# Layer 1's second product: earlier weight conversions, a third float64 tile, g loaded four steps ahead

## The chip, the core and the metric

The kernel runs on one core of a Trainium2 chip. The metric is the device time of one execution in microseconds (us). Five engines have a queue each and work through it in order: PE (TensorE, the matmuls; PEld is its weight load), DVE (VectorE), ACT (ScalarE), POOL (GpSimd) and SP (SyncE, here an issuer of DMAs). ACT issues DMAs too. An instruction that waits holds up all that is queued behind it on its engine.

## The reference

Attention with a sigmoid in place of the softmax, then two feed-forward layers over 1,792 tokens of 768 features, with 2,048 hidden features each:

```python
def _attn_ref(q, k, v):
    scores = scale * np.matmul(q, k.transpose(0, 1, 3, 2)) - np.log(S)
    attn = 1.0 / (1.0 + np.exp(-scores))
    return np.matmul(attn, v)

def _moe_ref(x, w_in, w_out):
    h = x @ w_in
    g = h * (1.0 / (1.0 + np.exp(-h)))
    return g @ w_out

def _moe2_ref(x, w_in, w_out, a, b):
    h = x @ w_in
    P = a[0] + a[1] * h + a[2] * h * h + a[3] * h ** 3
    Q = 1.0 + np.abs(b[0]) * np.abs(h) + np.abs(b[1]) * h * h
    return (P / (Q + 1e-06)) @ w_out
```

q, k and v are (4, 12, 448, 64): B = 4 batches of S = 448 tokens. The four weight matrices arrive as float64 numbers, and the kernel handles them as pairs of 32-bit words.

## The kernel before

**Precision.** A float32 operand is split into a high part (a cast to fp32r) and the low rest, and each product is three matmuls: high by high, high by low, low by high. `split` (L286) and `split2` (L290) make the high part on ACT (L287, L291) and the low part on DVE (L288, L292); `split_later` and `flush` (L296, L300) put the low parts behind other DVE work (L302).

**Conversions.** The weights come as 64 tiles of float64, 32 for each layer, each 768 KB. `conv` (L141) takes the oldest staged tile, makes float32 of it with one ACT instruction (L150) and four DVE instructions (L151, L152, L153, L156), stores the result of 384 KB to DRAM (L159, on SP) and issues the load of the next float64 tile (`conv_load`, L126, also on SP) into the staging tile it has freed. There are two staging tiles (`NST`). The order of the tiles is fixed: 16 of w_in1, 16 of w_out1, then layer 2's 32. Later the float32 tiles are loaded again: w_in1 into `wf` by `load_w1` (SP), w_out1 into `wos` by `load_wo1` (ACT's queue), layer 2's by `load_w2`.

**Stages.** First comes attention, 24 steps i. Then layer 1's first product by Strassen's scheme in 16 steps g of seven products each (`p1` to `p7`, L423 for the matmuls); step g sums and splits the weights for the next one (`sums_12`, `prep_...`) and loads those of g + 2. The silu of a result goes to DRAM as `gd`. Then layer 1's second product, which is where most of the change lies: 64 steps n, batch b = n // 16 by slice c = n % 16 of the hidden features. `second(n)` is 18 matmuls of 128x448 (L559 to L561), six groups that each add to one PSUM bank. In the first batch (the first block, n = 0 to 15) each step also needs its weights split (`split_wo1`), which stay in SBUF from then on. At the end of a block (n = 15, 31, 47, 63) `results1` copies six results from PSUM to SBUF and stores them as `xs`. Layer 2 follows, in which no weight is converted.

**Order of a step of the second product.** The code issues `load_g(n + 2)` (224 KB of `gd` into one of the nine `f448` slots, DMA on ACT's queue, L525), then `second(n)`, then `split_gd(n + 1)` (ACT L287, DVE L288), in the first block also `split_wo1(n + 1)` and `load_wo1(n + 5)`, then `results1` if a block ends, then `conv_to`, which converts as many tiles as an even pace asks for. At n = 2 `both`, `c21` and `c12` finish the first product's last results. At n = 49 the first loads for layer 2 are issued (four `load_w2`, three `load_x`); from n = 52 on each step holds a `split_x`, and two steps a `split_w` on POOL.

**How many conversions where.** 18 in attention, 10 in the Strassen steps (g = 0, 2, 4, 6 and 10 to 15), and 36 in the second product, n = 3 to 58 at an even pace, 9 of them in the first block: the last four of w_out1 and all of layer 2's.

The nine f448 slots and the staging tiles are rings: the slot that was put back first is taken first, whatever still reads it; the new user then waits.

Of the kernel before, what the change touches and what calls it, by code (L numbers as in the profile page):

```python
# [41 lines left out]
def attention_moe_moe(ctx: ExitStack, tc: tile.TileContext, q, k, v, w_in1, w_out1, w_in2, w_out2, a, b2, out):  # L42
# [23 lines left out]
    def fixed(nm, n, shape, dt, pool=cpool):  # L66
        return [pool.tile(shape, dt, tag=f"{nm}{i}", name=f"{nm}{i}") for i in range(n)]
# [10 lines left out]
    f_all = cpool.tile([P, 9 * S], F32, tag="f", name="f")  # L78
    f448 = Ring([f_all[:, i * S : (i + 1) * S] for i in range(9)])
    f2 = Ring([f_all[:, i * 2 * S : (i + 1) * 2 * S].rearrange("p (j s) -> p j s", j=2) for i in range(4)])  # L80
    xio = Ring(fixed("xio", 3, [P, BK], F32))
    stage = Ring(fixed("stg", NST, [P, DM, 2], I32))
    bits = Ring(fixed("bits", 3, [P, DM], F32))
    xs = [[dr_p.tile([P, NT], F32, tag=f"xs{m}_{d}", name=f"xs{m}_{d}") for d in range(KD)] for m in range(2)]
# [80 lines left out]
    def conv_to(count):  # L165
        while done["conv"] < min(count, len(order)):
            conv()
# [353 lines left out]
    def load_g(n):  # L521
        if n < B * KF:
            b, c = divmod(n, KF)
            gq[n] = f448.get()
            nc.scalar.dma_start(out=gq[n], in_=gd[c][b])  # L525

    def split_gd(n):
        if n < B * KF:
            t = gq.pop(n)
            gx[n] = hl.get()  # L530
            split(t, gx[n])
            f448.put(t)
# [4 lines left out]
    def load_wo1(c):  # L537
        if c < KF:
            wo_in[c] = wos.get()
            nc.scalar.dma_start(out=wo_in[c], in_=wd[0][c]["o"])  # L540

    def split_wo1(c):
        if c < KF:
            t = wo_in.pop(c)
            split2(t, woH[c], woL[c])
            wos.put(t)
# [6 lines left out]
    def second(n):  # L553
        b, c = divmod(n, KF)
        x = gx.pop(n)
        for d in range(KD):
            o = ybank(b, d)
            w = slice(d * P, (d + 1) * P)
            nc.tensor.matmul(o, woH[c][:, w], x[:, 0, :], start=(c == 0), stop=False)  # L559
            nc.tensor.matmul(o, woH[c][:, w], x[:, 1, :], start=False, stop=False)  # L560
            nc.tensor.matmul(o, woL[c][:, w], x[:, 0, :], start=False, stop=(c == KF - 1))  # L561
        hl.put(x)
# [15 lines left out]
    def load_w2(kind, c):  # L578
        nc.sync.dma_start(out=slot(kind, c), in_=wd[1][c][kind])
# [19 lines left out]
    def split_x(g, d):  # L599
        w = blocks[g][1]  # L600
        t = xf.pop((g, d))
        x = hx.get()
        nc.scalar.copy(x[:, 0, :w], t[:, :w])
        nc.vector.tensor_tensor(out=x[:, 1, :w], in0=t[:, :w], in1=x[:, 0, :w].bitcast(F32), op=ALU.subtract)
        xio.put(t)
        xs_hl[g, d] = x
# [136 lines left out]
    with tc.manual_schedule():  # L743
# [36 lines left out]
        for i in range(NPT):  # L780
            for h in range(2):
                if h == 0:
                    mix(i + 2)
                    load_v(i + 3)
                    load_qk(i + 4)
                attn_S(i, 2 * h, attn_QK(i, 2 * h))
                p = attn_QK(i, 2 * h + 1)
                if h == 0:
                    if i == 0:
                        attn_T(1, "k")  # L790
                    attn_T(i + 1, "q")
                else:
                    hl.put(st.pop(("k", i)), st.pop(("q", i)))
                    attn_T(i + 2, "k")
                attn_S(i, 2 * h + 1, p)
                behind(*((i, 0) if h else (i - 1, 1)))
                at_half = 2 * i + h - 2 * NPT
                if at_half >= -NOPS - 6:
                    next(first_ops, None)
                flush()  # L800
                if at_half == -8:
                    load_w1(0)
                    load_w1(1)
                if at_half == -5:
                    xk_s.close()
                    wr_p, wr_s = opened("wr")
                    wr.extend(fixed("wr", 4, [P, DM], F32R, wr_p))
                    wq.extend(fixed("wq", 6, [P, HM], F32R, wr_p))
                    prep_ij(0)
                    sums_12(0)  # L810
                if at_half == -3:
                    prep_s12(0)
                if at_half == -1:
                    prep_a22(0)
                if h == 0 and 0 < i < NPT - 5:
                    conv()
        for _ in first_ops:
            pass
# [25 lines left out]
        for g in range(NGR):  # L844
            was = g >= 1

            p1(g)
            flush()
            if was:
                keep(g - 1, "u3")  # L850
            if g >= 2:
                c12(g - 2)
            if g == HF:
                operands1_late("T3")
            if g == HF + 1:
                operands1_late("22")

            p2(g)
            flush()
            keep(g, "s1")  # L860
            if was:
                both(g - 1, "u3", "c")
            sums_34(g)
            if g == HF - 1:
                operands1_late("T2")

            if was:
                p4(g - 1)
                c22(g - 1)
            flush()  # L870
            both(g, "s1", "b")
            sums_12(g + 1)
            if was:
                fill(g)
            if g in (0, 2, 4, 6) or g > HF + 1:
                conv()

            p6(g)
            flush()
            c11(g)  # L880
            if was:
                c21(g - 1)
            prep_s3(g)
            if g == HF - 1:
                operands1_late("T1")
            if g == HF:
                operands1_late("T4 sums")
            if g == last:
                for n in range(4):
                    load_g(n)  # L890

            p5(g)
            flush()
            keep(g, "r")
            prep_ij(g + 1)
            if g:
                prep_a22(g)
            fill(g)
            if g == HF:
                operands1_late("T4")  # L900
            if g == last:
                split_wo1(0)
                load_wo1(4)
                split_gd(0)

            if was:
                p3(g - 1)
            flush()
            load_w1(g + 2)
            if g == HF - 1:  # L910
                operands1_late("T3 sums")
            if g == last - 1:
                kt_s.close()
                wos_p, wos_s = opened("wos", side="right")
                wos.put(*fixed("wos", 4, [P, DM], F32, wos_p))
                for c in range(4):
                    load_wo1(c)
            if g == last:
                split_wo1(1)
                load_wo1(5)  # L920
                split_gd(1)

            p7(g)
            flush()
            if was:
                both(g - 1, "r", "c")
            prep_s12(g + 1)
            prep_s4(g)
# [17 lines left out]
        split_wo1(2)  # L946
        load_wo1(6)
        split_gd(2)
        NL1 = B * KF
        todo = len(order) - done["conv"]  # L950
        for n in range(2, NL1):
            load_g(n + 2)
            second(n)
            if n == 2:
                c21(last)
                both(last, "r", "c")
                c12(last)
            split_gd(n + 1)
            if n + 1 < KF:
                split_wo1(n + 1)  # L960
                load_wo1(n + 5)
            if n == KF - 1:
                wos_s.close()
                l2_p = ctx.enter_context(tc.tile_pool(name="l2a", bufs=1, side="right", reuse_waits="tile"))
                hx.put(*fixed("hx", KD, [P, 2, BK], F32R, l2_p))
                wi_f.extend(fixed("wif", 4, [P, DM], F32, l2_p))
            if n % KF == KF - 1:
                results1(n // KF)
            conv_to(len(order) - todo + todo * (n - 1) // (NL1 - 7))
            m = n - (NL1 - KF)  # L970
            if m == 1:
                whr.put(w0[:2], w0[2:])
                for c in range(4):
                    load_w2("i", c)
                for d in range(HK):
                    load_x(0, d)
            if 4 <= m < 4 + KD:
                split_x(0, m - 4)
                if m - 4 < HK:
                    load_x(0, m - 4 + HK)  # L980
            if m in (KF - 6, KF - 4):
                split_w("i", (m - KF + 6) // 2)
        assert done["conv"] == len(order)
        wo_s.close()
        xa_s.close()
        l2_p = ctx.enter_context(tc.tile_pool(name="l2b", bufs=1, reuse_waits="tile"))
# [16 lines left out]
        wo_f.extend(slots["o", c] for c in range(KF))  # L1003
        whr.put(more_wh[:2], more_wh[2:])
        for t in list(stage.free):
            t = t.bitcast(F32).rearrange("p e t -> p (e t)")
            xio.put(*(t[:, i * BK : (i + 1) * BK] for i in range(2 * DM // BK)))
        for c in range(KF):
# [40 lines left out]
```

## Time and profile before

| | us |
|---|---|
| median of three runs | 1128.04 |
| lowest and highest of the runs | 1127.06, 1131.84 |
| the profiled execution | 1133.58 |
| its span in the trace | 1131.8 |
| attention until about | 182 |
| the Strassen product until | 387.13 |
| the second product, to the end of its last step | 658.62 |
| layer 2 until | 1131.8 |

The rows that are needed stand in a section of their own below. The page's busy times tell which engine has no time to spare over the span; the windows tell that for a stage; the waits tell what an engine stood still for; the timeline names single instructions, with the idle time before them and what ended it in brackets.

### The profile page before, as it was taken

What the parts mean: (1) busy time and instruction counts of PE and PEld (TensorE: products, weight loads), DVE (VectorE), ACT (ScalarE), POOL (GpSimd) and SP (SyncE); (2) the same over time, 40 slices, a digit from 0 to 9 for tenths busy, and PEclk for the clock granted to TensorE, in tenths of its full rate; (3) what the DMA queues carried; (4) which work ended last, traced back from release to release, by engine and by line L of the source; (5) the groups of instructions that cost most, each with busy time, mean ns of one, the idle gap of its engine ahead of it and who ended that gap; (6) DMA issues with size and microseconds to landing.
All of it is one profiled execution on the core that took longest, in us unless ns stands there. A gap on an engine that the chain in (4) does not pass through costs nothing.

```text
span 1131.8 us, 15809 instructions
## 1 busy us (share of the span) xinstructions
PE 1096.3 (97%) x5822; PEld 913.8 (81%) x5822; DVE 862.2 (76%) x1028; ACT 636.3 (56%) x1035; POOL 341.8 (30%) x246
## 2 busy tenths in 40 slices
PE   9999999999999898999998899999999999999997
PEld 5554456999998787889987788888999888889997
DVE  4668855778876747767675758888999988798996
ACT  6778885666655533323322345546666765566664
POOL 2111210000000000000000136656777666566774
PEclk9999999999999999999999999999999999999999
DMA  9999962766556848888889573010101010001001
GB/s 253 261 263 248 286 216 98 256 211 212 168 191 216 280 165 285 266 280 277 302 270 330 173 285 154 1 35 8 57 1 47 12 41 1 29 15 56 1 1 42
DMA packets 100349, 177.96 MB, mean 157 GB/s; under 512 B 8368, under 2 KB 74416, under 8 KB 100272
## 3 DMA queue, kind: packets, MB, share of 16 engines
q1 hardware_dynamic: 88048, 155.38, 42.7%
q10 hardware_dynamic: 12160, 21.57, 5.9%
q8 instruction: 46, 0.75, 0.3%
q14 instruction: 31, 0.25, 0.1%
q0 software_dynamic: 64, 0.00, 0.0%
HBM read 123.31 MB, written 53.61 MB: 156 GB/s over the span
## 4 chain that ended last, share of the span: by engine, by line
PE 80%; DVE 8%; DMA 7%; ACT 2%; issue 2%; ACTq 1%; SPq 0%; POOL 0%; DVEq 0%; POOLq 0%
PE acc L690 14%; PE acc L423 10%; PE acc L693 7%; PE hb L621 7%; PE hb L619 7%; PE hb L620 7%; PE hb L264 6%; PE pair L246 5%; PE hb L423 4%; PE acc L560 3%; PE acc L561 3%; PE acc L559 3%; DMA f<-gd 3%; PE hb L236 2%; DVE bits L153 1%
## 5 line engine op out<-in xcount | busy, mean ns | idle before, releaser
L292 POOL TENSOR_TENSOR w<-wif,w 128x768 fp32r<-128x768 f32 x33 | 62.0, 1879 | 486.5 <-ACT w L291 482.0
L257 ACT ACTIVATE f<-pair,nls 112x896 f32<-112x896 f32 x96 | 96.7, 1012 | 26.8 <-PE pair L246 26.8
L560 PE MATMUL acc<-xa,woH 128*128 128x448 f32 x252 | 94.3, 374 | 5.5 <-DVE xa L288 5.5
L559 PE MATMUL acc<-xa,woH 128*128 128x448 f32 x252 | 93.9, 372 | 3.6 <-ACT xa L287 3.5
L561 PE MATMUL acc<-xa,woL 128*128 128x448 f32 x252 | 93.4, 371 | 0.0
L150 ACT ACTIVATE bits<-stg 128x768 f32<-128x768 f32 x64 | 57.7, 902 | 63.3 <-DMA stg<-in_moe_w_in_dram 38.7
L647 DVE RECIPROCAL stg<-stg 128x512 f32<-128x512 f32 (+1 forms) x28 | 84.9, 3032 | 0.0
L634 ACT ACTIVATE stg<-hb,absb 128x512 f32<-128x512 f32 (+1 forms) x44 | 28.0, 637 | 98.2 <-PE hb L621 98.2
L264 PE MATMUL hb<-f,vs 112*64 112x448 f32 x384 | 82.5, 551 | 0.0
L287 ACT CAST xa<-f 128x448 fp32r<-128x448 f32 x64 | 36.0, 562 | 81.6 <-DMA f<-gd 65.9
L246 PEld LDWEIGHTS pair<-xa,xa 64*112 64x112 f32 x576 | 47.2, 173 | 38.5 <-issue 32.4
L246 PE MATMUL pair<-xa,xa 64*112 64x448 f32 x576 | 71.7, 381 | 0.0
L423 PE MATMUL acc<-xb,wr 128*128 128x448 f32 x315 | 67.8, 366 | 0.0
L292 POOL TENSOR_TENSOR wh<-wif,wh 128x768 fp32r<-128x768 f32 x31 | 57.4, 1851 | 26.4 <-DVE xio L639 23.6
L151 DVE TENSOR_SCALAR bits<-bits 128x768 f32<-128x768 f32 x64 | 35.7, 557 | 37.9 <-ACT bits L150 37.6
L156 DVE SCALAR_TENSOR_TENSOR bits<-stg,bits 128x768 int32<-128x768 int32 x64 | 62.8, 981 | 2.2
L423 PEld LDWEIGHTS acc<-xb,wr 128*128 128x128 f32 x315 | 59.0, 188 | 5.5 <-issue 0.7
L153 DVE SCALAR_TENSOR_TENSOR bits<-stg,bits 128x768 int32<-128x768 int32 x64 | 61.4, 959 | 2.2
L288 DVE TENSOR_TENSOR xa<-f,xa 128x448 fp32r<-128x448 f32 x64 | 39.0, 620 | 30.1 <-ACT xa L287 30.1
L690 PE MATMUL acc<-w,hx 128*128 128x512 f32 x174 | 61.4, 393 | 0.0
L690 PE MATMUL acc<-wh,hx 128*128 128x512 f32 x171 | 60.3, 393 | 0.0
L292 POOL TENSOR_TENSOR w<-wof,w 128x768 fp32r<-128x768 f32 x32 | 59.3, 1852 | 0.4 <-ACT w L291 0.2
(195 smaller groups left out, 3188.8 us busy)
## 6 DMA issues: line engine op xcount, KB each, us to landing
stg<-in_moe_w_in_dram SPq DMA_DIRECT2D x32, 768.0 KB, 6.4
stg<-in_moe_w_out_dram SPq DMA_DIRECT2D x32, 768.0 KB, 6.2
gd<-f SPq DMA_DIRECT2D x64, 224.0 KB, 4.9
f<-gd ACTq DMA_DIRECT2D x64, 224.0 KB, 4.5
wf<-w0i SPq DMA_DIRECT2D x32, 384.0 KB, 6.0
w0i<-bits SPq DMA_DIRECT2D x16, 384.0 KB, 2.9
w0o<-bits SPq DMA_DIRECT2D x16, 384.0 KB, 2.6
wos<-w0o ACTq DMA_DIRECT2D x16, 384.0 KB, 4.6
```

Of the source, the lines that this page charges most:

```text
L246: nc.tensor.matmul(p[:CP, j, :S], K[rows[j], a_, c * CP : (c + 1) * CP], Q[rows[j], b_, :], start=(n == 0), stop=(n == 2),)
L257: nc.scalar.activation(t[:CP], p[:CP, :, :S], AF.Sigmoid, bias=nls[:CP], scale=QKSCALE)
L264: nc.tensor.matmul(pav[0][j * D : (j + 1) * D, :S], vs[i][:, j, c * D : (c + 1) * D], t[:CP, j], start=(c == 0), stop=(c == NCH - 1),)
L292: (eng or nc.vector).tensor_tensor(out=lo, in0=src, in1=h.bitcast(F32), op=ALU.subtract)
L423: nc.tensor.matmul(o, w_[:, w], x[:, i_, :], start=first and kk == 0 and n_ == 0, stop=kk == HK - 1 and n_ == 2, skip_group_check=not first,)
L559: nc.tensor.matmul(o, woH[c][:, w], x[:, 0, :], start=(c == 0), stop=False)
L560: nc.tensor.matmul(o, woH[c][:, w], x[:, 1, :], start=False, stop=False)
L561: nc.tensor.matmul(o, woL[c][:, w], x[:, 0, :], start=False, stop=(c == KF - 1))
L619: nc.tensor.matmul(o, wh[:, w], x[:, 0, :wd_], start=first, stop=False)
L620: nc.tensor.matmul(o, wh[:, w], x[:, 1, :wd_], start=False, stop=False)
L647: nc.vector.reciprocal(t0, t1)
L690: nc.tensor.matmul(acc[t][:, :BK], a_, w_[:, :BK], start=first, stop=last)
```

## The change

**Conversions.** Attention holds two more (i = 19, 20), the Strassen steps two more (g = 1 and g = 9), so that 32 are done ahead of the second product: all of layer 1's. In the second product three stand in the first block (n = 5, 9, 13), and 29 in n = 17 to 51: every step but n = 22, 27, 32, 37, 42 and 47. Thus 32 instead of 36, and none behind n = 51.

**A third float64 tile.** The three `xio` tiles are allocated as one, and that stands in as a third staging tile (`more`) from n = 2 on, until layer 2's `load_x` takes the three tiles back.

**Loads of g.** `load_g(n + 4)` instead of `load_g(n + 2)`; two more are issued ahead of the loop.

**Order.** At n = 2 the splits for n = 3 stand ahead of `c21`, `both` and `c12`. `load_x` starts at n = 53 instead of 49, `split_x` at n = 55 instead of 52; `load_w2` stays.

```diff
-    xio = Ring(fixed("xio", 3, [P, BK], F32))
+    x_all = cpool.tile([P, 3, BK], F32, tag="xio", name="xio")
+    xio = Ring([x_all[:, i, :] for i in range(3)])
...
-                if h == 0 and 0 < i < NPT - 5:
+                if h == 0 and 0 < i < NPT - 3:
                     conv()
...
-            if g in (0, 2, 4, 6) or g > HF + 1:
+            if g in (0, 1, 2, 4, 6) or g > HF:
                 conv()
...
+        load_g(4)
+        load_g(5)
         NL1 = B * KF
-        todo = len(order) - done["conv"]
+        more = x_all.rearrange("p a b -> p (a b)").bitcast(I32).rearrange("p (e t) -> p e t", t=2)
+        stage.put(more)
+        conv_load()
+        first, slow, end = done["conv"], KF - 2, NL1 - 12
+
+        def conv_by(n):
+            if n <= KF:
+                return first + (n - 1) // 4
+            return first + slow // 4 + -(-(n - KF) * (len(order) - first - slow // 4) // (end - KF))
+
         for n in range(2, NL1):
-            load_g(n + 2)
+            load_g(n + 4)
             second(n)
+            split_gd(n + 1)
+            if n + 1 < KF:
+                split_wo1(n + 1)
+                load_wo1(n + 5)
             if n == 2:
                 c21(last)
                 both(last, "r", "c")
                 c12(last)
-            split_gd(n + 1)
-            if n + 1 < KF:
-                split_wo1(n + 1)
-                load_wo1(n + 5)
...
-            conv_to(len(order) - todo + todo * (n - 1) // (NL1 - 7))
+            conv_to(conv_by(n))
             m = n - (NL1 - KF)
...
             if m == 1:
                 whr.put(w0[:2], w0[2:])
                 for c in range(4):
                     load_w2("i", c)
+            if m == 5:
                 for d in range(HK):
                     load_x(0, d)
-            if 4 <= m < 4 + KD:
-                split_x(0, m - 4)
-                if m - 4 < HK:
-                    load_x(0, m - 4 + HK)
+            if 7 <= m < 7 + KD:
+                split_x(0, m - 7)
+                if m - 7 < HK:
+                    load_x(0, m - 7 + HK)
```

From L81 on the lines of the changed kernel are one higher, so L151 there is L150 here. PE's order is unchanged.

DVE in the Strassen step g = 1, before: the last two sums of the next weights (`sf`), the low part of an operand (`xa`), the low part of `wq`, which p7 of this step reads, and the next operand.

```order
L309 TENSOR_TENSOR sf_253<-wf_1_250 128x384
L306 TENSOR_TENSOR sf_253<-sf_253,wf_0_249 128x384
L288 TENSOR_TENSOR xa_216<-T_1957,xa_216 128x448
L302 TENSOR_TENSOR wq_1844<-sf_254,wq_1843 128x384
L288 TENSOR_TENSOR xa_219<-xio_63,xa_219 128x448
```

The same place now:

```order
L310 TENSOR_TENSOR sf_251<-wf_1_248 128x384
L307 TENSOR_TENSOR sf_251<-sf_251,wf_0_247 128x384
L289 TENSOR_TENSOR xa_214<-T_1969,xa_214 128x448
L152 TENSOR_SCALAR bits_64<-bits_64 128x768
L153 TENSOR_SCALAR bits_64<-bits_64 128x768
L154 SCALAR_TENSOR_TENSOR bits_64<-stg_63,bits_64 128x768
L157 SCALAR_TENSOR_TENSOR bits_64<-stg_63,bits_64 128x768
L303 TENSOR_TENSOR wq_1856<-sf_252,wq_1855 128x384
L289 TENSOR_TENSOR xa_217<-xio,xa_217 128x448
```

A whole conversion stands between `xa` and `wq`. Its store and the 768 KB load that follows it also come ahead of the next weights' loads (`wf`) in SP's queue.

ACT in the first block, before: three steps, each with the high part of g (`xa`), the high part of the weights (`woH`), the load of later weights (`wos`) and of a later g (`f<-gd`); the first of the three steps has a conversion (`bits`).

```order
L287 CAST xa_220<-f 128x448
L291 CAST woH_3660<-wos_3462 128x768
L540 DMA wos_3462<-w0o_162 128x768
L150 ACTIVATE bits_67<-stg_64 128x768
L525 DMA f<-gd_0_105 128x448
L287 CAST xa_221<-f 128x448
L291 CAST woH_3662<-wos_3463 128x768
L540 DMA wos_3463<-w0o_164 128x768
L525 DMA f<-gd_0_109 128x448
L287 CAST xa_222<-f 128x448
L291 CAST woH_3664<-wos_3464 128x768
L540 DMA wos_3464<-w0o_166 128x768
```

The same engine in the same block now:

```order
L288 CAST xa_218<-f 128x448
L292 CAST woH_3686<-wos_3488 128x768
L541 DMA wos_3488<-w0o_160 128x768
L526 DMA f<-gd_0_111 128x448
L288 CAST xa_219<-f 128x448
L292 CAST woH_3688<-wos_3489 128x768
L541 DMA wos_3489<-w0o_162 128x768
L526 DMA f<-gd_0_115 128x448
L288 CAST xa_220<-f 128x448
L292 CAST woH_3690<-wos_3490 128x768
L541 DMA wos_3490<-w0o_164 128x768
```

None of these three steps has a conversion now, and `f<-gd` is for two steps further on.

ACT at the end of the first block, before: three of the six copies of `results1` (to slots `f_60`), then the loads of g for n = 18, 19 and 20 with the high parts for n = 17 and 18.

```order
L567 COPY f_60<-hb0_281 128x448
L567 COPY f_60<-acc1_1967 128x448
L567 COPY f_60<-acc3_1969 128x448
L525 DMA f_60<-gd2_1_90 128x448
L287 CAST xa8_224<-f_60 128x448
L150 ACTIVATE bits0_66<-stg0_64 128x768
L525 DMA f_60<-gd3_1_94 128x448
L287 CAST xa0_216<-f_60 128x448
L150 ACTIVATE bits1_67<-stg1_65 128x768
L525 DMA f_60<-gd4_1_98 128x448
```

Now:

```order
L568 COPY f_60<-hb0_279 128x448
L568 COPY f_60<-acc1_1979 128x448
L568 COPY f_60<-acc3_1981 128x448
L526 DMA f_60<-gd4_1_96 128x448
L288 CAST xa8_222<-f_60 128x448
L526 DMA f_60<-gd5_1_100 128x448
L288 CAST xa0_214<-f_60 128x448
L151 ACTIVATE bits2_66<-stg0_62 128x768
L526 DMA f_60<-gd6_1_104 128x448
```

The first load behind the copies is that of n = 20 (`gd4_1`), and it takes the slot from which `results1` stores its first result; before, the load of n = 20 stood two steps later. The high part for n = 17 is queued behind it, and in the later blocks those for n = 33 and n = 49 likewise.

## Rows read from the trace of the kernel before

**Rows 1.** The page: busy time of each engine over the span.

```profile
PE 1096.3 (97%) x5822; PEld 913.8 (81%) x5822; DVE 862.2 (76%) x1028; ACT 636.3 (56%) x1035; POOL 341.8 (30%) x246
```

**Rows 2.** Windows: bounds, length; busy us (instructions) by engine; clock, DMA share, GB/s.

```profile
387.13:467.07 79.94, 68.86 (x307) 59.39 (x307) 51.25 (x71) 30.86 (x48) 0.00 (x0) 0.96 0.68 229
467.07:529.07 62.00, 60.17 (x289) 53.84 (x288) 41.09 (x59) 18.34 (x30) 0.00 (x0) 1.00 0.84 275
529.07:588.59 59.52, 59.52 (x289) 54.06 (x288) 40.90 (x59) 18.39 (x30) 0.00 (x0) 1.00 0.86 288
588.59:658.62 70.03, 62.20 (x290) 54.96 (x288) 40.95 (x56) 20.84 (x35) 4.61 (x2) 0.98 0.71 238
658.62:1131.80 473.18, 466.34 (x2497) 413.49 (x2495) 414.12 (x342) 284.82 (x490) 304.56 (x190) 1.00 0.14 46
```

**Rows 3.** Waits of PE, second product: line, releaser, total us, times, longest.

```profile
PE acc L560 <- DVE xa L288: 6.1, 8, 2.4
PE hb L560 <- DVE xa L288: 4.7, 5, 1.3
PE acc L559 <- ACT xa L287: 3.5, 1, 3.5
PE hb L559 <- DVE f L309: 2.8, 1, 2.8
```

**Rows 4.** Timeline, DVE and PE, first block: start, duration, instruction [idle before].

```profile
411.89 0.56 DVE L151 TENSOR_SCALAR bits<-bits 128x768 f32<-128x768 f32 x1 [1.32 <-ACT bits L150]
...
414.95 0.62 DVE L288 TENSOR_TENSOR xa<-f,xa 128x448 fp32r<-128x448 f32 x1
415.49 0.95 DVE L292 TENSOR_TENSOR woL<-wos,woH 128x768 fp32r<-128x768 f32 x1
...
410.41 0.36 PE L559 MATMUL hb<-xa,woH 128*128 128x448 f32 x1
...
414.06 0.36 PE L559 MATMUL hb<-xa,woH 128*128 128x448 f32 x1
415.62 0.47 PE L560 MATMUL hb<-xa,woH 128*128 128x448 f32 x1 [1.20 <-DVE xa L288]
```

**Rows 5.** Timeline of ACT, first block: conversions of two steps running.

```profile
420.08 0.89 ACT L150 ACTIVATE bits<-stg 128x768 f32<-128x768 f32 x1 [1.40 <-DVE woL L292]
...
425.95 0.91 ACT L150 ACTIVATE bits<-stg 128x768 f32<-128x768 f32 x1 [2.44 <-DVE woL L292]
```

**Rows 6.** Windows of 10 us, columns as in rows 2.

```profile
536.00:546.00 10.00, 10.00 (x50) 9.09 (x49) 6.59 (x11) 2.76 (x5) 0.00 (x0) 1.00 0.92 330
616.00:626.00 10.00, 9.54 (x36) 7.83 (x36) 4.96 (x8) 5.17 (x9) 0.00 (x0) 0.83 0.85 302
666.00:676.00 10.00, 9.18 (x46) 7.40 (x45) 9.89 (x8) 7.31 (x12) 8.27 (x5) 1.00 1.03 401
```

**Rows 7.** Timeline of ACT and PE: the longest wait of block four.

```profile
613.96 0.62 ACT L603 CAST hx<-xio 128x512 fp32r<-128x512 f32 x1 [5.58 <-DMA xio<-xs]
...
615.10 0.47 PE L559 MATMUL acc<-xa,woH 128*128 128x448 f32 x1 [3.53 <-ACT xa L287]
```

**Rows 8.** Waits of PE in attention, then in the Strassen product.

```profile
PE hb L236 <- DVE xa L239: 2.7, 5, 0.6
...
PE hb L423 <- DVE wq L302: 1.3, 1, 1.3
```

**Rows 9.** Timeline of DVE and PE at g = 1 of the Strassen product.

```profile
203.21 0.62 DVE L288 TENSOR_TENSOR xa<-T,xa 128x448 fp32r<-128x448 f32 x1
203.75 0.55 DVE L302 TENSOR_TENSOR wq<-sf,wq 128x384 fp32r<-128x384 f32 x1
...
204.07 0.98 PE L423 MATMUL hb<-xa,wq 128*128 128x448 f32 x4
```

**Rows 10.** results1's stores (L568): first ones of block two; all, issue to landing.

```profile
527.75 2.42 SPq L568 DMA_DIRECT2D xs<-f  x4
...
DMA to landing us min/median/max: 1.9/6.1/8.4
```

More of the change, by code (lines that the diff above doesn't have):

```diff
@@ L968, in attention_moe_moe @@
                 results1(n // KF)
-            conv_to(len(order) - todo + todo * (n - 1) // (NL1 - 7))
+            conv_to(conv_by(n))
             m = n - (NL1 - KF)
+            if m == 4:
+                assert done["conv"] == len(order)
             if m == 1:
@@ L974, in attention_moe_moe @@
                     load_w2("i", c)
+            if m == 5:
                 for d in range(HK):
                     load_x(0, d)
-            if 4 <= m < 4 + KD:
-                split_x(0, m - 4)
-                if m - 4 < HK:
-                    load_x(0, m - 4 + HK)
+            if 7 <= m < 7 + KD:
+                split_x(0, m - 7)
+                if m - 7 < HK:
+                    load_x(0, m - 7 + HK)
             if m in (KF - 6, KF - 4):
                 split_w("i", (m - KF + 6) // 2)
-        assert done["conv"] == len(order)
         wo_s.close()
@@ L1005, in attention_moe_moe @@
         for t in list(stage.free):
+            if t is more:
+                continue
             t = t.bitcast(F32).rearrange("p e t -> p (e t)")
```

## The prediction, made before the changed kernel was run

> **What bounds the kernel now.** I read the page's busy times first. PE is busy 97% of the span, and the next engine, DVE, 76% [rows 1]: time can be won only where PE waits, or where its matmuls run slowly. The windows by stage come next. After 658.62 PE is busy 466.34 of 473.18 us [rows 2], and the change leaves that stage alone. The stretch to look at is the second product, 387.13 to 658.62. There I need the price of a step with nothing late: steps 4 and 5 begin 3.65 us apart, at 410.41 and 414.06 [rows 4]. A block of 16 steps is then 58.4 us. The first block also holds two products of the stage before, which have the matmuls of one step: 62.05. Measured are 79.94, 62.00, 59.52 and 70.03 us [rows 2], so the blocks lose 17.9, 3.6, 1.1 and 11.6 us, **34.2 us in all**. That is the most that the second product can give.
>
> What is lost, and to whom, the waits of PE tell. Nearly all are for operands on their way through ACT and DVE: the low part of g (L288) 6.1 and 4.7 us, its high part (L287) once for 3.5, and 2.8 at the start for the sum `f` that frees a PSUM bank [rows 3]. The clock is the rest: the window that begins a microsecond after the wait of 3.5 us shows 0.83 of full speed over 10 us, so (1 - 0.83) x 10 = 1.7 us more [rows 6].
>
> **The first block.** The timeline shows what a conversion does. Its four DVE instructions run from 411.89 to the `xa` at 414.95, 3.06 us, and only then come the low parts that PE needs; PE stands for 1.20 us at 415.62 [rows 4]. On ACT the conversion's first instruction begins only once the low weights are done, at 420.08 and, a step later, at 425.95 [rows 5]: two steps with conversions running are 5.87 us apart. Less the 3.06 us, a step without one is about 2.8, under PE's 3.65. So each conversion in this block puts the chain 5.87 - 3.65 = 2.2 us behind, and each free step wins 0.85 back. Nine conversions in the 13 steps from n = 3 would cost 9 x 2.2 - 4 x 0.85 = 16.4, less the lead that g had. Of 17.9 us lost, 2.8 + 1.7 = 4.5 is the start (wait and clock), which the change doesn't touch, and 13.4 comes from this. Three conversions four steps apart fall behind by 2.2 and win 3 x 0.85 = 2.6 back; with g loaded two steps earlier PE should hardly stand. I leave 1.2 us (0 to 4).
>
> **The other blocks.** Block two loses 3.6 and block three 1.1; of that I leave 1.7, since the matmuls of block three run 3.72 us a step, without waits [rows 2], and that remains. In block four two things go: the high part of g for n = 54 is queued on ACT behind a `split_x` whose load is late by 5.58 us, and PE waits 3.53 [rows 7], with 1.7 of slow clock after it; and a conversion late in the block, beside the first splits on POOL, makes PE wait 2.4 [rows 3]. The changed kernel has no conversion after n = 51 and starts the `split_x` three steps later. I leave 0.3.
>
> **A new wait at the ends of blocks.** The order of ACT shows the load for n = 20, 36 and 52 right behind the copies of `results1`, into the slot whose store was just issued. ACT stands until that store has landed, with the high part for the next step but one behind it. Block two's first store was issued at 527.75, and these stores take 1.9 to 8.4 us to land, 6.1 at the median [rows 10]: to 533.9. With 0.6 us for a cast (0.62 at 613.96 [rows 7]) PE would have its operand at 534.5. It needs it one step after 529.07, at 532.8 (3.72 a step [rows 2]): 1.7 us late at the median, 4.0 at 8.4, not at all at 1.9. DMA is busier in the new blocks, so I take 2.6, plus 0.9 for an even chance that the clock falls (1.7 us [rows 6]): **3.5 us at n = 33 and 3.5 at n = 49**, each 0 to 5.6. At n = 17 it is nothing, since few conversions load DMA there. [...] Here PE waited up to 2.4 us and 3.5 us [rows 3], and only of the longer does a row show the clock.
>
> **The DMA queues.** Steps 17 to 48 hold 26 conversions, 0.786 MB in and 0.393 out each, 32 loads of g at 0.229 MB and 2.75 MB of results: 40.7 MB in 32 x 3.7 = 118.4 us, 344 GB/s. Block three moved 288 GB/s at a DMA share of 0.86 [rows 2], 335 if it were full; the window from 536 shows 330 at 0.92 [rows 6], or 359. At 335 the bytes take 121.5 us, 3.1 too long; at 359 nothing. I take **1.5 us** (0 to 8, which is 322 GB/s). The third staging tile and g four steps ahead let queued work ride over late loads; they move no byte more. The Trainium skill, DMA: Bandwidth & Descriptors, section Specifications, gives a core about 358 GB/s of HBM; by that the drag is nothing and rival D below is out. The trace neither sits at that limit nor obeys it: 401 GB/s for 10 us from 666 [rows 6].
>
> **What the earlier conversions cost.** Attention: PE has waited 2.7 us in five places for DVE, up to 0.6 each [rows 8]; two more conversions, 0.7 (0 to 1.2). The late Strassen steps: conversions that begin one step earlier, where one had made PE wait 1.3 [rows 8]: 0.7 (0.3 to 1.3). At g = 1 a conversion goes between `xa` (203.21) and `wq` (203.75, ends 204.30), which p7 reads: its matmuls begin at 204.07 as one row of four [rows 9], so the third starts at about 204.5, and 0.2 us are spare. 3.06 - 0.2 = **2.9 us** of wait. SP's queue holds the conversion's store and a 768 KB load ahead of the weights for g = 3, whose sums come ahead of the next `wq`: nothing at best, another 2.9 at worst; 1.5. Together 5.8 us (3 to 9).
>
> **The sum.** After: 4.5 + 1.2 + 1.7 + 0.3 + 3.5 + 3.5 + 1.5 = 16.2 us lost in the second product, 18.0 less than 34.2; with 5.8 lost ahead of it the change wins 12.2 us. The profiled execution took 1133.58 us (span 1131.8), so its like would be 1121.4. It lies 5.5 above the median of the three runs, 1128.04; less 12.2 that is 1115.8, and as part of the 5.5 may sit in the very waits that go, I say **1117 us**. The terms' own ends don't all fall together: 1110 to 1124.
>
> **Rivals.**
> A is this forecast.
> B: the stores at the block ends land in 2 to 4 us, and the weights at g = 3 are in time. For: the conversion issued just ahead of those stores is gone from n = 47. Against: their median of 6.1 us [rows 10]. After: 9.2 us lost, 25.0 won, 4.3 paid: 1107.
> C: the gain is given back to DMA. Staged tiles come late, ACT waits for them in order, and g's high part waits behind. Six waits like the 1.7 us worked out above make the drag 10 us, not 1.5. Won 9.5, paid 5.8: 3.7 us, 1124, which is no change. For: the window from 616, at 0.85 share, still had only 302 GB/s [rows 6].
> D: the same queue, at its old rate. The second and third blocks can't take 344 GB/s, and PE is paced by DMA. It decides from 296 GB/s down: 40.7 MB then take 137.5 us, 19.1 over the 118.4, against the 1.5 in the sum; 12.2 won turn to 5.4 lost. At block three's 288 it is 141.3 us, 22.9 over, 9.2 lost: 1137, slower. For: 275 and 288 GB/s are the best that whole blocks have shown [rows 2]. Against: their share was 0.84 and 0.86, and ten microseconds at 0.92 gave 330.
> That the change doesn't do what it says is excluded by the order, which shows conversions and loads where they should be.
>
> **How the numbers follow.** A 0.50, B 0.14, C 0.24, D 0.12. A measurement of this kernel can tell about 0.5% from no change: below 1122.4 is faster, above 1133.7 slower. Faster: 0.44 of A, all of B, 0.02 of C, 0.60. Same: 0.06 of A, 0.22 of C, 0.02 of D, 0.30. Slower: the rest of D, 0.10. The range, 1108 to 1129, takes in A and C and leaves out D and about half of B.
>
> **What would show it.** In the profile after: PE's wait for `wq` near 204, about 2.9 us (if none, 3 us of my costs are wrong); no period of 5.87 us in two steps running of the first block; a row of ACT at n = 33 and 49 that waits for the store of `results1`, with PE late by 1 to 4 us; DMA share near 0.95 or over in blocks two and three, at 330 GB/s or more. A step of over 3.8 us through those blocks, with ACT waiting for staged tiles, means C or D. If PE still stands in the first block for 5 us or more, my reading of its chain was wrong.

## The result

The changed kernel takes **1113.50 us** at the median of four runs (1109.78 to 1114.97), the kernel before, run beside it, 1129.03 (1127.06 to 1131.84). The ratio is **0.9856, with a 95% interval of 0.9823 to 0.9889**: 1.4% faster. Forecast were 1117 us and a range of 1108 to 1129. The profiled execution took 1114.97 us, its span is 1113.2.

The kernel before had medians of 1131.0 to 1132.6 us in the sessions that follow, so kernels of different sessions are compared by their ratios to it.

### The profile page after: what moved, and what is told of

It reads as the page before. It is cut to its first block, busy times and chain, and to the rows that moved or that the text cites. A ratio compares the mean times of both kernels' runs of the same rounds, so it can differ in the third digit from the quotient of the medians.

```text
span 1113.2 us, 15823 instructions
## 1 busy us (share of the span) xinstructions
PE 1092.7 (98%) x5822; PEld 914.2 (82%) x5822; DVE 859.9 (77%) x1028; ACT 634.3 (57%) x1035; POOL 341.7 (31%) x246
## 4 chain that ended last, share of the span: by engine, by line
PE 88%; DVE 6%; DMA 4%; issue 1%; ACT 1%; SPq 0%; POOL 0%; ACTq 0%; DVEq 0%; POOLq 0%
PE acc L691 14%; PE acc L424 9%; PE acc L694 7%; PE hb L622 7%; PE hb L620 7%; PE hb L621 7%; PE hb L265 6%; PE acc L561 5%; PE acc L560 5%; PE acc L562 5%; PE pair L247 5%; PE hb L424 3%; PE hb L237 2%; DMA wf<-w0i 2%; PE hb L560 2%; PE hb L562 2%
## 5 line engine op out<-in xcount | busy, mean ns | idle before, releaser
L560 PE MATMUL acc<-xa,woH 128*128 128x448 f32 x252 | 92.3, 366 | 0.0
L561 PE MATMUL acc<-xa,woH 128*128 128x448 f32 x252 | 92.3, 366 | 0.0
L151 ACT ACTIVATE bits<-stg 128x768 f32<-128x768 f32 x54 | 48.7, 903 | 52.6 <-DMA stg<-in_moe_w_in_dram 23.1
L293 POOL TENSOR_TENSOR wh<-wof,wh 128x768 fp32r<-128x768 f32 x32 | 59.2, 1851 | 0.1
L691 PE MATMUL acc<-wh,hy 128*128 128x512 f32 x165 | 58.6, 396 | 0.0
L691 PE MATMUL acc<-w,hy 128*128 128x512 f32 x162 | 57.3, 396 | 0.0
L240 DVE TENSOR_TENSOR xa<-hb,xa 128x448 fp32r<-128x448 f32 x48 | 29.7, 620 | 34.0 <-ACT xa L239 33.7
L289 DVE TENSOR_TENSOR xa<-f,xa 128x448 fp32r<-128x448 f32 x64 | 42.0, 666 | 17.9 <-ACT xa L288 17.8
```

What stands on the lines that cost most here:

```text
L293: (eng or nc.vector).tensor_tensor(out=lo, in0=src, in1=h.bitcast(F32), op=ALU.subtract)
L691: nc.tensor.matmul(acc[t][:, :BK], a_, w_[:, :BK], start=first, stop=last)
```

## The profile after

The page's busy times, as in [rows 1]:

```profile
PE 1092.7 (98%) x5822; PEld 914.2 (82%) x5822; DVE 859.9 (77%) x1028; ACT 634.3 (57%) x1035; POOL 341.7 (31%) x246
```

The windows of the four blocks of the second product and of what follows, columns as in [rows 2]; the bounds are the starts of n = 0, 16, 32 and 48 and the end of n = 63:

```profile
395.76:462.98 67.22, 65.02 (x307) 58.66 (x306) 35.63 (x49) 25.98 (x42) 0.00 (x0) 0.97 0.66 223
462.98:522.50 59.52, 59.52 (x289) 54.06 (x288) 46.33 (x67) 19.70 (x32) 0.00 (x0) 1.00 0.90 324
522.50:581.79 59.29, 58.71 (x289) 54.02 (x288) 49.28 (x71) 20.47 (x33) 0.00 (x0) 1.00 0.98 344
581.79:640.16 58.37, 58.37 (x289) 54.10 (x288) 28.84 (x40) 17.01 (x31) 3.84 (x2) 1.00 0.50 166
640.16:1113.20 473.04, 466.29 (x2497) 413.55 (x2495) 413.98 (x342) 284.75 (x490) 304.22 (x190) 1.00 0.14 46
```

Against 62.05 and three times 58.4 us the blocks now lose 5.2, 1.1, 0.9 and 0.0: **7.2 us instead of 34.2**. But the stage begins at 395.76 and not at 387.13: **8.6 us are paid ahead of it**. 27.0 less 8.6 is the 18.4 by which the second product ends earlier; layer 2 takes 473.0 us as before (473.2).

PE's waits, with the second product's rows of [rows 3] in view: line, releaser, us in total, times, longest.

```profile
PE hb L424 <- DVE wq L303: 3.8, 2, 2.5
...
PE hb L560 <- DVE f L310: 2.2, 1, 2.2
PE acc L424 <- DVE wq L303: 1.5, 2, 1.3
...
PE acc L561 <- DVE xa L289: 0.6, 1, 0.6
```

Of the waits of [rows 3] only 2.2 us at the start and 0.6 at n = 33 are left. New at the top is `wq`, 3.8 us, in the Strassen product, where [rows 8] had 1.3.

The timeline of DVE at g = 1, as in [rows 9], with PE's matmul behind it:

```profile
204.24 0.62 DVE L289 TENSOR_TENSOR xa<-T,xa 128x448 fp32r<-128x448 f32 x1
204.77 0.56 DVE L152 TENSOR_SCALAR bits<-bits 128x768 f32<-128x768 f32 x1
...
206.95 0.96 DVE L157 SCALAR_TENSOR_TENSOR bits<-stg,bits 128x768 int32<-128x768 int32 x1
207.82 0.55 DVE L303 TENSOR_TENSOR wq<-sf,wq 128x384 fp32r<-128x384 f32 x1
...
208.43 1.86 PE L424 MATMUL hb<-xa,wq 128*128 128x448 f32 x4 [2.48 <-DVE wq L303]
```

The conversion stands from 204.77 to 207.9 between `xa` and `wq`, and PE waits 2.48 us.

The stores of `results1`, as in [rows 10], and on ACT the one cast that waits for such a store:

```profile
DMA to landing us min/median/max: 1.9/2.2/4.4
...
520.21 3.46 SPq L569 DMA_DIRECT2D xs<-f  x6
...
582.82 0.57 ACT L288 CAST xa<-f 128x448 fp32r<-128x448 f32 x1 [0.90 <-DMA xs<-f]
```

They land in 2.2 us at the median, not 6.1. What differs is how shortly ahead of them a load was issued on SP. In the kernel before it was 0.4 us earlier, ahead of the store at 527.75 [rows 10]:

```profile
527.32 0.37 SPq L137 DMA_DIRECT2D stg<-in_moe_w_out_dram  x1
```

Now the last 768 KB load stands 9.2 us ahead of the store at 520.21, and 8.7 and 4.1 us at the other two block ends. Over the first three block ends of all thirteen kernels whose traces this document uses, the first store landed in 5.5 to 8.2 us where such a load was issued under 0.7 us ahead (12 cases), in 6.0 and 6.3 where it was 1.7 and 1.0 us, and in 1.9 to 4.9 where it was 3 us or more (25 cases).

## The experiments

Each is given with its edit, the expectation on record, and what was measured. Blocks are compared by their length in the profile, as above.

**The conversion at g = 1.**

```diff
-            if g in (0, 1, 2, 4, 6) or g > HF:
+            if g in (0, 2, 4, 6) or g > HF:
                 conv()
```

> The changed kernel without the conversion at g = 1 of the Strassen product; 31 tiles are converted ahead of the second product, and the one left over goes to its steps. Theory: that conversion alone makes PE wait 2.48 us near 208 us and run slowly for 1.5 us behind it, so 4.0 us go, and the time is 1109.5 us against 1113.5. Rival: DVE is as full at g = 2 and the weights there are late in any case; the wait moves there and at most 1 us is won, 1112.5 to 1113.5.

Measured: 1108.71 us, ratio 0.9808 (0.9775 to 0.9842). The interval overlaps that of the changed kernel, so the trace has to decide, and there the theory holds: the product in which PE waited takes 2.11 us instead of 5.84 (1.82 undisturbed), 3.7 us less, and g = 2 shows no wait. The profiled execution is 6.2 us shorter than that of the changed kernel. The rest is not this conversion's: the step n = 0 takes 7.66 us instead of 9.56, the matmul spacing told of in the last section gives some 4 us, and other waits cost part of that again.

**g two steps ahead again.**

```diff
-        load_g(4)
-        load_g(5)
...
-            load_g(n + 4)
+            load_g(n + 2)
```

> The changed kernel with g loaded two steps ahead, as before the change, all else kept. Theory: the few conversions in the first block made the gain; the first block stays free of waits, blocks two and three lose at most 3 us to g that comes late behind the denser loads: 1114 to 1117. Rival: the distance of the loads made it; ACT's waits for g (65.9 us before the change) come back and hold up PE in every block, as before: 1120 to 1127.

Measured: 1116.44 us, ratio 0.9877 (0.9839 to 0.9915), as the theory has it; the interval holds the changed kernel's ratio. The blocks take 67.57, 59.52, 59.29 and 58.36 us, those of the changed kernel within 0.4. The first block is not quite free of waits, though: its step n = 0 happens to be 1.5 us shorter, and n = 12 and 13 take 5.02 and 4.40 us instead of 3.72. ACT's waits for g are back, as the rival said, 52.5 us from the second block on, and PE does not feel them there. With three staging tiles and few early conversions the distance of g's loads is worth some 2 us in the trace, and nothing that the times can tell.

**Two staging tiles again.**

```diff
-        stage.put(more)
-        conv_load()
```

> The changed kernel with two staging tiles, as before the change, all else kept. Theory: with 1.18 MB of conversion traffic in four of five steps a tile comes 6 to 7 us after its issue, so two tiles give at most one conversion in about 4 us; ACT waits for staged tiles with the casts of g behind it, and blocks two and three lose 5 to 10 us: 1118 to 1124. Rival: g four steps ahead and the lead of PE's operands cover that, the third tile is worth nothing: 1113 to 1115.

Measured: 1139.96 us, ratio 1.0103 (1.0066 to 1.0141): slower than before the change. The theory's mechanism is there, with three to five times the price. The windows of the blocks, and what PE waits for from the second block on:

```profile
395.56:460.36 64.80, 62.26 (x307) 57.39 (x306) 35.95 (x50) 25.94 (x42) 0.00 (x0) 1.00 0.65 219
460.36:520.78 60.42, 59.44 (x289) 53.78 (x289) 43.20 (x62) 19.07 (x32) 0.00 (x0) 1.00 0.86 278
520.78:594.08 73.30, 64.41 (x289) 57.06 (x288) 51.19 (x73) 21.06 (x34) 0.00 (x0) 0.93 0.86 281
594.08:663.52 69.44, 62.00 (x290) 55.61 (x289) 31.03 (x44) 17.11 (x31) 3.83 (x2) 0.95 0.55 183
...
PE acc L561 <- DVE xa L289: 9.0, 10, 2.2
PE acc L560 <- ACT xa L288: 8.4, 2, 5.2
...
stg<-in_moe_w_out_dram SPq DMA_DIRECT2D x13, 768.0 KB, 6.4
stg<-in_moe_w_in_dram SPq DMA_DIRECT2D x12, 768.0 KB, 6.1
```

The last two lines are the float64 loads issued between 460 and 600 us: their number, size and median us from issue to landing.

Blocks three and four lose 14.9 and 11.0 us. Block four has few conversions left to do by its plan, but they come late. ACT stands for staged tiles; the copies of `results1`, and then the block-end wait of my prediction, join in:

```profile
518.67 0.90 ACT L151 ACTIVATE bits<-stg 128x768 f32<-128x768 f32 x1 [4.76 <-DMA stg<-in_moe_w_in_dram]
...
520.77 0.55 ACT L568 COPY f<-acc 128x448 f32<-128x448 f32 x1
523.95 0.91 ACT L151 ACTIVATE bits<-stg 128x768 f32<-128x768 f32 x1 [2.63 <-DMA stg<-in_moe_w_out_dram]
530.73 0.36 ACTq L526 DMA_DIRECT2D f<-gd  x1
531.13 0.56 ACT L288 CAST xa<-f 128x448 fp32r<-128x448 f32 x1 [6.26 <-DMA xs<-f]
...
531.74 0.74 PE L560 MATMUL acc<-xa,w 128*128 128x448 f32 x1 [3.15 <-ACT xa L288]
```

ACT waits 6.26 us for the store behind `f<-gd`, and PE waits for it; at the next block end ACT waits 9.3. PE's waits of 16.3 us in these two blocks and a clock of 0.93 and 0.95 (5.1 and 3.5 us over them) make up 24.9 of the 25.9 us. DMA is not full: 281 GB/s at a share of 0.86, where the changed kernel moves 344 at 0.98. What lacks is a load in flight. An estimate from rows: a tile is taken up for 6.3 us while its load lands and for 4.0 us of conversion (0.9 on ACT, 3.06 on DVE [rows 4, rows 5]), so two tiles allow one conversion in 5.1 us, and this pace asks for 26 in 32 steps of 3.65, one in 4.5.

**The places of the conversions alone.**

```diff
-                if h == 0 and 0 < i < NPT - 5:
+                if h == 0 and 0 < i < NPT - 3:
...
-            if g in (0, 2, 4, 6) or g > HF + 1:
+            if g in (0, 1, 2, 4, 6) or g > HF:
...
-            conv_to(len(order) - todo + todo * (n - 1) // (NL1 - 7))
+            conv_to(conv_by(n))
```

> The kernel before with only the places of the conversions changed (20 in attention, 12 in the Strassen steps, 3 in the first block, 29 in n = 17 to 51); two staging tiles, g two steps ahead, split_x at its old steps. Theory: the first block's 13.4 us and the late conversion's 2.4 us are won by that alone, 8.6 us are paid ahead of the second product, and the wait behind split_x (3.5 + 1.7) stays: 1129 - 15.8 + 8.6 = 1122, 1119 to 1124. Rival: without the third tile and the earlier loads of g the denser conversions stall blocks two and three by as much as the first block wins: 1127 or more.

Measured: 1149.38 us, ratio 1.0172 (1.0132 to 1.0212). The rival is right, by more than it said. The blocks take 73.85, 63.13, 75.80 and 67.82 us. So the new places of the conversions alone make the kernel 1.7% slower; with the experiment before, which took away the third tile alone, this says that the pace behind the first block is not to be had with two tiles.

**The old order at n = 2.**

```diff
         for n in range(2, NL1):
...
+            if n == 2:
+                c21(last)
+                both(last, "r", "c")
+                c12(last)
             split_gd(n + 1)
```

> The changed kernel with the old order at n = 2: c21, both and c12 ahead of the splits for n = 3. Theory: ACT then stands some 5 us for the sum that c12 needs, with the casts for n = 3 behind it, and the lead that the first block needs for its three conversions is gone: 4 to 6 us lost, 1118 to 1120. Rival: three conversions in 14 steps leave room enough, the lead is won back at 0.85 us a step, and nothing is lost: 1113 to 1115.

Measured: 1116.51 us, ratio 0.9851 (0.9823 to 0.9879), which is the changed kernel's. The theory's 4 to 6 us did not come. The rival's nothing is not quite right either: the first block takes 66.92 us against 67.22, but the changed kernel ran it at the slower spacing of the last section. Beside steps of 3.65 us the steps n = 7 and n = 11 take 4.94 and 4.62 here, 2.3 us more, of which PE waits 1.2; in the changed kernel and three others with its order and its three conversions there (without the conversion at g = 1, with two tiles, with the short matmul) these steps are as long as their neighbours. This is one trace, and the times can't tell 2.3 us.

**The order at n = 2 alone**, the same edit the other way, on the kernel before.

> The kernel before with only the order at n = 2 changed: the splits for n = 3 stand ahead of c21, both and c12. Theory: nine conversions put the chain 16 us behind in any case, so a lead of one step wins 2 to 4 us: 1125 to 1127 against 1129. Rival: the 5.6 us for which ACT stands there are what starts the first block's waits; 5.6 us and more are won: 1123 or less.

Measured: 1124.41 us, ratio 0.9925 (0.9896 to 0.9953), with the kernel before at 1132.60 beside it: 8.2 us won (5.3 to 11.8 by the interval), what the rival asked for. The timeline of ACT in the kernel before shows what goes:

```profile
403.97 0.58 ACT L442 ACTIVATE f<-f 128x448 f32<-128x448 f32 x1 [5.59 <-DVE f L309]
404.46 0.55 ACT L287 CAST xa<-f 128x448 fp32r<-128x448 f32 x1
404.91 0.83 ACT L291 CAST woH<-wos 128x768 fp32r<-128x768 f32 x1
```

The silu of `c12` waits 5.59 us for a sum of DVE's, and the casts for n = 3 are queued behind it. The first block takes 72.63 us instead of 79.94. But 3.0 of these 7.3 us lie in the step n = 0, ahead of the place that was edited. The windows of n = 0 and of n = 1 to 15, in the kernel before and in this one:

```profile
387.13:397.64 10.51, 7.50 (x28) 6.26 (x28) 5.64 (x9) 4.48 (x8) 0.00 (x0) 0.84 0.72 256
397.64:467.07 69.43, 61.36 (x280) 53.14 (x279) 45.61 (x62) 26.38 (x40) 0.00 (x0) 0.98 0.67 225
...
386.57:394.10 7.53, 5.75 (x28) 5.00 (x27) 4.17 (x8) 4.58 (x9) 0.00 (x0) 1.00 0.79 294
394.10:459.20 65.10, 58.92 (x281) 51.85 (x279) 45.60 (x62) 25.63 (x39) 0.00 (x0) 1.00 0.74 248
```

At n = 0 PE waits 1.8 us and the clock stays full; in the kernel before it waits 2.8 us and the clock is 0.84 over the step. Both kernels run the same instructions there, and no run shows that the order has to do with it. Behind it 4.3 us are won, which is nearer the theory's 2 to 4. So this order costs some 4 us beside the many conversions of the old pace, and 2.3 beside three.

**An even pace.**

```diff
         def conv_by(n):
-            if n <= KF:
-                return first + (n - 1) // 4
-            return first + slow // 4 + -(-(n - KF) * (len(order) - first - slow // 4) // (end - KF))
+            return first + max(0, n - 2) * (len(order) - first) // (end - 3)
```

> The changed kernel with its 32 remaining conversions at an even pace over n = 4 to 51, nine of them in the first block instead of three. Theory: each conversion there costs the chain of ACT and DVE 2.2 us that the free steps win back at 0.85, so the first block loses 8 to 12 us more, and the other blocks nothing: 1121 to 1126. Rival: the new order and g four steps ahead gave the first block its room, not the number of conversions: 1113 to 1117.

Measured: 1122.51 us, ratio 0.9917 (0.9888 to 0.9946): the theory, a little under its price. The first block takes 73.71 us, 6.5 more than the changed kernel's; the others 59.32, 58.37 and 59.30. At the spacing of this run it is 7.5 us, in the steps n = 9, 11 and 12, which take 5.55, 5.48 and 7.40 us instead of 3.65. By the order of ACT eight conversions belong to the steps up to n = 15 and the ninth to n = 16, so this is the price of five more.

**An even pace with two tiles**, both of the edits above.

> The changed kernel with the 32 remaining conversions at an even pace over n = 4 to 51 and with two staging tiles. Theory: two tiles give about one conversion in 4.5 to 5 us; the even pace asks for one in 5.5 us, so here the third tile is worth little, and the time is that of the even pace with three tiles within 4 us: 1122 to 1127. Rival: the third tile is needed at any pace, since loads land 6 us and more after their issue: 1135 or more, as with two tiles at the denser pace.

Measured: 1127.53 us, ratio 0.9969 (0.9947 to 0.9991). Nearer the theory: by the ratios the third tile is worth 0.5% here, some 6 us, a little more than the 4 allowed, against 2.5% (28 us) at the changed kernel's pace. The 5.1 us estimated above lie between the two paces, one conversion in 4.5 us and one in 5.5.

**The later split_x alone**, on the kernel before.

```diff
-            if 4 <= m < 4 + KD:
-                split_x(0, m - 4)
+            if 7 <= m < 7 + KD:
+                split_x(0, m - 7)
```

> The kernel before with only load_x and split_x moved to n = 53 and 55 on. Theory: the wait of 3.5 us behind split_x at n = 54 and its 1.7 us of slow clock go, nothing else moves: 5.2 us less, 1124 against 1129. Rival: conversions go on to n = 58 in this kernel, and the later splits meet them and the first splits on POOL there; the wait moves to n = 57 to 60, and the time stays at 1128 to 1131.

Measured: 1128.50 us, ratio 0.9960 (0.9942 to 0.9978). That lies between the two, and the interval, 2.5 to 6.6 us, holds the theory's 5.2. The profile leans to the rival: n = 53 and 54 no longer take 7.34 and 6.11 us, but n = 56 takes 7.99, and block four is 67.91 us instead of 70.03. In the changed kernel, with the conversions out of its way, block four loses nothing; the earlier end of the conversions without the move was not tried.

**A version from what the traces showed.** No conversion at g = 0 and 1, the others of the Strassen steps behind `wq`'s low part, the sum that frees a PSUM bank earlier, five conversions in n = 4 to 16 (four of them in the first block).

```diff
-            if g in (0, 1, 2, 4, 6) or g > HF:
-                conv()
...
             p5(g)
             flush()
+            if g in (2, 4, 6) or g > HF:
+                conv()
             keep(g, "r")
...
             if g == last:
+                both(g - 1, "r", "c")
                 split_wo1(1)
...
-            if was:
+            if was and g < last:
                 both(g - 1, "r", "c")
...
-                return first + (n - 1) // 4
+                return first + (n - 1) // 3
...
```

> The changed kernel with four edits that the traces point to: no conversions at g = 0 and 1; those of the other Strassen steps behind the low part of wq instead of ahead of it; the last both of the Strassen product ahead of the splits for the second product, so that a PSUM bank comes free earlier; five conversions in the first block (n = 4, 7, 10, 13, 16) instead of three. Theory: PE's waits for wq (1.3 us at g = 0, 2.5 and 1.5 of slow clock at g = 1, some 2 in the late steps) and the 2.2 us at the start of the second product with its slow clock go: 1113.5 - 1.3 - 4.0 - 2 - 3.5 = 1102.7. Rival: conversions behind wq push back wr, which the next step's first product reads, and five conversions make the first block wait: 1108 to 1112, no better than without the conversion at g = 1 alone.

Measured: **1101.02 us, ratio 0.9737 (0.9704 to 0.9770)**, faster than both. The page's busy times, and PE's largest waits over the whole span:

```profile
PE 1083.0 (99%) x5822; PEld 911.7 (83%) x5822; DVE 861.5 (78%) x1028; ACT 635.4 (58%) x1035; POOL 341.0 (31%) x246
...
PE hb L237 <- DVE xa L240: 3.3, 6, 0.6
...
PE hb L622 <- POOL wh L293: 0.8, 1, 0.8
PE hb L560 <- ACT xa L288: 0.7, 1, 0.7
PE acc L561 <- DVE xa L289: 0.7, 1, 0.7
```

No wait for `wq` is left and no wait of over 0.8 us behind 182 us. The profiled execution is 14.9 us shorter than that of the changed kernel; some 5.6 of them are the matmul spacing of the last section, so the four edits gave about 9, a little less than the theory's 10.8. Only the dropped conversion at g = 1 was also tried by itself.

**A short matmul**, told of in the last section.

```diff
+        if n in (16, 32, 48):
+            nc.tensor.matmul(ybank(b, 0)[:, :64], woH[c][:, :P], x[:, 0, :64], start=True, stop=True)
```

> The changed kernel with one matmul of 64 columns more, ahead of the first of n = 16, 32 and 48; its result is overwritten. It asks about the two spacings of matmuls, 202.7 and 206.7 ns, that all traces so far show in stretches of tens of us. Theory: the spacing is a state that PE keeps until something breaks its row of matmuls, so it can change at these three places without any wait. Rival: it changes only with a wait, or it is set by what DVE, ACT and the DMAs do meanwhile, and the three places show nothing. Time 1110 to 1116 either way.

Measured: 1112.22 us in one run. It settles nothing: at all three places the spacing was 202.7 ns already, and it stayed.

## Why the prediction was right, and where its sum was off

The time was 3.5 us under the forecast, and the two halves of the sum were each off by more: 27.0 us won where I had 18.0, 8.6 paid where I had 5.8. Execution against execution the miss is 6.4 us, 1114.97 against 1121.4; that the forecast came as near as 3.5 is in part luck.

- **The start**, 4.5: 2.20 us of wait and a clock of 0.83 over 10 us, 1.7. Right; the first block's 5.2 are this and the spacing.
- **The first block**, 1.2 left: no wait is left in it behind its start. The outcome was right and the reason half of it. I put all 13.4 us to nine conversions, and by the order of ACT the ninth belongs to n = 16, outside the block. The even pace gives 7.5 us for five more than three; the order at n = 2, which the front of this document shows in the diff, is not in my sum, and it is worth some 4 us by itself in the kernel before. Undone in the changed kernel it costs 2.3 in the one trace there is.
- **The block ends**, 3.5 each at n = 33 and 49: the step that failed. The wait at n = 49 is on ACT as described, 0.90 us, and PE does not feel it; at n = 33 PE waits 0.58 for a low part behind a conversion on DVE. The step took the landing time of the kernel before, where a 768 KB load had been issued just ahead of these stores, and a busier DMA as a reason for more. Rival B's first half was the truth, 1.9 to 4.4 us, and for the reason it gave: that load is gone. With two tiles a load stands 0.5 us ahead of the stores again, and the same waits are there, at 6.26 and 9.3 us, so mechanism and place were right and the landing wrong.
- **DMA**, 1.5: nothing. Block two moved 324 GB/s at a share of 0.90 and block three 344 at 0.98, about what 40.7 MB in 118.4 us asks for, and 50 us of block two had 361 at 1.00 (below). C and D did not come, but not for the reason given, that the bytes fit. They fit with two tiles too, and that kernel is 2.5% slower. The step priced a rate, and the limit was how many loads are under way. "They move no byte more" was true of the third tile, and it was no reason to give it no term.
- **The late block**, 0.3: right, 0.0. The later `split_x` by itself wins 2.1 of the 11.6 us there; with no conversions behind n = 51 as well nothing is lost.
- **Attention**, 0.7: 1.06.
- **g = 1**, 2.9 and 1.5: the wait was 2.48, and the clock fell behind it, 1.5 us that I had not put there; the weights for g = 3 came in time, for which I had taken 1.5. Together 4.0 against 4.4, right by luck.
- **Late Strassen steps**, 0.7: under 0.8.
- **Not in the sum**: 2.8 us between 193 and 340, where each matmul comes 4 ns later than before and, g = 1 apart, no wait is seen. That is the excess of the 8.6.

A window of 50 us of the changed kernel, in block two:

```profile
465.00:515.00 50.00, 50.00 (x244) 45.41 (x243) 43.29 (x62) 16.36 (x26) 0.00 (x0) 1.00 1.00 361
```

The Trainium skill, DMA: Bandwidth & Descriptors, section Specifications, has about 358 GB/s of HBM for a core. The trace's sustained figure over 50 us is close to that, 361 at a full share, though 10 us at 401 were seen [rows 6]. By the page, D was to be left out; it did not come.

## What to carry to other kernels

Where a stage converts or copies ahead of a busy engine, count first how many loads are in flight: staging tiles against the time for landing and conversion, and look at the rate after that. Here the denser pace without the extra tile turned a gain of 1.4% into a loss of 1.0%. Work that is moved to an earlier stage is best put behind the instruction on its engine that the next matmul waits for, not ahead of it; together with the conversions at g = 0 and 1 dropped and one sum moved forward that was worth another 1.2%, part of it the spacing of matmuls below. And the worth of an edit depends on the others: undo each singly and try each alone. The third tile was worth 28 us at one pace and 6 at another, the order 4 us in the old kernel and 2 in the new. When two executions are compared block by block, look first at the parts that both run alike.

## What the hardware showed that was not expected

**Two spacings of the same matmuls.** Stretches without a wait run at 202.7 or at 206.7 ns a matmul, and keep to it for tens of us. The windows from 220 to 330, the Strassen product, for the kernel before, the changed kernel, the one with near loads of g, whose program is the same up to there, and the last version:

```profile
220.00:330.00 110.00, 110.00 (x544) 101.95 (x543) 84.24 (x146) 67.70 (x127) 0.00 (x0) 1.00 0.59 201
```

```profile
220.00:330.00 110.00, 110.00 (x534) 99.91 (x533) 89.00 (x151) 66.73 (x125) 0.00 (x0) 1.00 0.63 209
```

```profile
220.00:330.00 110.00, 109.49 (x541) 101.16 (x540) 89.27 (x152) 67.37 (x126) 0.00 (x0) 1.00 0.64 214
```

```profile
220.00:330.00 110.00, 110.00 (x544) 101.89 (x544) 86.92 (x149) 69.44 (x129) 0.00 (x0) 1.00 0.63 211
```

PE is busy all 110 us at full clock in three of them, and gets 544, 534 and 544 matmuls done; 541 in the other, with some half us without one. Between 182 and 665 us the changed kernel spends about 292 us in the slow way, the kernel before 113, the one without the conversion at g = 1 82, and the last version none. At 1.9% these are 5.6, 2.2, 1.6 and 0 us; some of the 5 us by which runs of one kernel differ may be this. Three executions with the same program up to n = 2 (the changed kernel, near loads of g, the short matmul) first held the slow spacing from 193 to 340, 192 to 205 and 193 to 354, with a wait or two in between. So it is not the program alone that decides. Most changes fall at a break, a matmul that comes 0.1 us or more late or the clock's return to full; but near 482.7 us with the order alone and near 440 with near loads of g the spacing changes with no matmul later than 207 ns, and other breaks change nothing, those of the short matmul among them. What sets the spacing is open.

**The clock after waits of about 2 us.** At the start of the second product PE waits 2.20 us in the changed kernel and 1.91 in the one without the conversion at g = 1. Windows of 10 us, over the waits at g = 1 and at the start in the one, at the start in the other:

```profile
206.00:216.00 10.00, 7.57 (x30) 6.87 (x31) 8.70 (x14) 2.83 (x6) 0.00 (x0) 0.83 0.73 237
396.00:406.00 10.00, 7.80 (x31) 6.68 (x30) 5.45 (x9) 5.16 (x9) 0.00 (x0) 0.83 0.91 316
```

```profile
391.00:401.00 10.00, 8.09 (x40) 7.15 (x40) 5.70 (x9) 5.17 (x9) 0.00 (x0) 1.00 0.97 346
```

The granted clock is 0.83, 0.83 and 1.00. The first two are means of both levels: behind the wait the matmuls come 373 ns apart, at 1.2 GHz, and then 207 ns, at 2.4. In the kernel before a wait of 2.4 us left the clock full while this one of 2.20 did not, and with two tiles one of 2.54 us at the same place left it full too (1.00 over its first block, above). A wait's length alone does not tell whether the 1.7 us follow.
